# The request order of four weight slabs and one transpose in a two-layer transformer kernel

## Chip, cores, metric

The kernel runs on one core of one Trainium2 chip. The metric is the device time of one execution in microseconds (us).

## The reference, cut to what matters

```python
x = A_x                                              # 2048 tokens x 1024, bf16
x = x + _A_ref(_layernorm(x), A_wqkv, A_wo)          # attention over 8 dilated positions
x = x + _B_ref(_layernorm(x), W_gate, W_up, W_down)  # relu(x Wg) * (x Wu), then Wd; F = 3584
... # both lines once more
```

## The kernel before

The tokens are worked on in blocks of 512, that is, four tiles of 128 rows. Weights come as slabs of 1 MB through a ring of five buffers. The program is written as a list of events with plan times; the events are sorted and emitted, so a plan time settles only the order of instructions on each engine. It isn't a time on the chip. All loads and transposes below are issued by one queue, that of SyncE (SP).

```python
def sp_dma(dst, src, transpose=False):
    start = nc.sync.dma_start_transpose if transpose else nc.sync.dma_start
    ...                                   # each is issued after the one before it

def want_gu(n, at, gap):                  # gate and up slabs, with the time their use ends
    for s in range(NSG):
        cols = slice(s * SLAB, min((s + 1) * SLAB, F))
        end = at + gap * min(4 * (s + 1), FC)
        want(("g", n, s), wg_v[:, :, cols], end)
        want(("u", n, s), wu_v[:, :, cols], end)

def slab_events(events):                  # a slab is asked for when the slab five before it ends
    for i, (key, src, _) in enumerate(slab_plan):
        ...                               # f: takes a ring buffer, sp_dma(tv, src)
        events.append((slab_plan[i - RING][2] + 0.3 if i >= RING else 0.1 * i, f))

def ln2(n, ats, turn_at=None, dve=()):    # second norm: stats, apply, transpose of each tile
    stats, apply, turn, hold = ln_steps(n, "b", False, dve)
    for t, a in enumerate(ats):
        ev.append((a, stats[t]))
        ev.append((a + 4.0, apply[t]))
        if turn_at is None:               # only the first block: one transpose per tile
            ev.append((a + (7.5 if t == TPB - 1 else 6.0), turn(t)))
    ...

# gate and up: every matmul reads the transposed norm of all four tiles
for nm in ("g", "u"):
    for kc in range(KC):
        mm(acc[:], lhsT=slab[(nm, n, s4)][:, kc, jl * P:(jl + 1) * P], rhs=ln["xnT"][:, :, kc, :], ...)

# plan of the stretch in question
want_v("v123", t_v3 + GRP * KC / 2, t_gu0)   # two V slabs, ends 141.3 and 148.2
want_wo(0, t_v3, t_v3)                       # two slabs of the output projection, end 134.3
spread(wo_steps(0), t_wo0, 2 * GRP)
ln2(0, [...], None, (2, 3))                  # tiles 0 and 1 on ScalarE, 2 and 3 on VectorE
spread(v_steps(3, ln_a[3], "v123"), t_v3, GRP)   # V projection of block 3
...                                              # then gate and up of block 0, from t_gu0 on
```

In the text, T0 to T3 are the transposes of the first block's four tiles (256 KB each), g00, g01, g02 the gate slabs 0, 1, 2 of block 0, and u00, u01 its up slabs.

## Time and profile before

| what | value |
|---|---|
| time, median of 3 runs | 1651.05 us (1649.98 to 1651.11) |
| span of the profiled run | 1648.9 us (1648.95 with one more digit) |
| TensorE (PE) busy | 98% |
| its longest wait | 11.0 us, before the first gate matmul |

The page of the kernel before, its first lines (busy us of each engine, share of the span, instructions). PE is TensorE, PEld its weight loads, DVE is VectorE, ACT ScalarE, POOL GpSimd:

```profile
span 1648.9 us, 18636 instructions
PE 1620.7 (98%) x7576; PEld 777.8 (47%) x7576; DVE 1059.4 (64%) x918; ACT 512.2 (31%) x1057; POOL 267.3 (16%) x220
```

PE bounds the kernel, and what can be won by reordering is its idle time. The table of waits of the kernel before, with its PE lines (waiting instruction, releaser, total us, times, longest):

```profile
engine line waited for: us in total, times, longest us
...
PE acc_g L118 <- issue: 11.0, 1, 11.0
PE tp L294 <- DVE xn_first L276: 9.0, 1, 9.0
...
```

The 9.0 us are the start of the program. The 11.0 us are one gap; "issue" says that PE waited for nothing that this profile shows, so the releaser has to be looked for elsewhere. The timeline of PE of the kernel before shows where the gap lies (start, duration, what; idle time before it in brackets):

```profile
135.26 14.17 PE L118 MATMUL acc_v<-xnT_a,w_v 128*128 128x512 bf16 x64
160.44 3.57 PE L118 MATMUL acc_g<-xnT_b,w_g 128*128 128x512 bf16 x8 [11.01 <-issue]
163.81 2.38 PE L118 MATMUL acc_u<-xnT_b,w_u 128*128 128x512 bf16 x8
166.02 1.89 PE L118 MATMUL acc_g<-xnT_b,w_g 128*128 128x512 bf16 x8
```

The V projection ends at 149.43, the first gate matmul starts at 160.44. The first two groups of eight take 5.58 us (160.44 to 166.02), while two later ones take 3.45. The timeline of SP of the kernel before, in the same stretch (start and length of an issue, not of the transfer):

```profile
145.32 1.23 SPq L107 DMA_TRANSPOSE xnT_b<-xn_b  x1
146.65 0.53 SPq L107 DMA_DIRECT2D w_u<-in_B_W_up_dram  x1
147.27 0.59 SPq L107 DMA_DIRECT2D w_g<-in_B_W_gate_dram  x1
147.96 4.41 SPq L107 DMA_TRANSPOSE xnT_b<-xn_b  x1
152.49 0.51 SPq L107 DMA_DIRECT2D w_u<-in_B_W_up_dram  x1
153.10 2.85 SPq L107 DMA_TRANSPOSE xnT_b<-xn_b  x1
156.48 0.38 SPq L107 DMA_DIRECT2D w_g<-in_B_W_gate_dram  x1
```

These are T1, u01, g02, T2, u00, T3, g01. The view of the tile xnT_b, cut to 153 to 156 us, gives T3's time from issue to landing in the kernel before:

```profile
DMA to landing us min/median/max: 7.2/7.2/7.2
```

So T3 lands at 153.10 + 7.2 = 160.3, and PE starts 0.1 us later: T3 ends the gap. Three slabs stand between T1 and T3. The window table of the kernel before gives the clock and the load of the DMA engines (busy time and instructions of PE, PEld, DVE, ACT, POOL; granted clock, that is, the share of full speed at which TensorE was let run; mean share of the 16 DMA engines; GB/s):

```profile
152.00:155.00 3.00, 0.00 (x0) 0.00 (x0) 2.90 (x2) 0.00 (x0) 0.00 (x0) 0.92 1.19 329
155.00:158.00 3.00, 0.00 (x0) 0.00 (x0) 2.96 (x3) 0.00 (x0) 0.00 (x0) 0.50 1.09 320
158.00:161.00 3.00, 0.56 (x2) 0.28 (x3) 3.00 (x2) 0.41 (x1) 0.00 (x0) 0.50 1.15 334
```

The DMA engines are full in these windows (a share of 1.09 to 1.19), so everything that stands ahead of T3 delays it. The clock has fallen to 0.50 by the time PE starts again: this explains the slow first groups (5.58 us, against 3.45 at a clock of 1.00).

### The profile page before, as it was taken

Reading aid. Unit: us, or ns where it says so; the run is one execution under the profiler, and the core shown is the slowest. Engines: PE = TensorE matmul, PEld = TensorE weight load, DVE = VectorE, ACT = ScalarE, POOL = GpSimd, SP = SyncE. Lnnn points to the kernel's source line nnn. Section 1 sums busy time; section 2 is a strip of 40 time slices with the busy share of each in tenths; the row PEclk is TensorE's granted clock in tenths of the full one; section 3 lists DMA queues with packets and bytes.
Section 4 is the critical chain, followed back from the end, with each engine's and each line's share of the span. In section 5 each row is a group of like instructions: output and inputs, shape, how many; then the busy total and the mean of one; then the engine's idle time right before and its main releaser. Section 6 shows DMA issues by size and latency. Waiting matters only on the chain.

```text
span 1648.9 us, 18636 instructions
## 1 busy us (share of the span) xinstructions
PE 1620.7 (98%) x7576; PEld 777.8 (47%) x7576; DVE 1059.4 (64%) x918; ACT 512.2 (31%) x1057; POOL 267.3 (16%) x220
## 2 busy tenths in 40 slices
PE   7997999999999999999999999999999999999999
PEld 4553445444454445444454444544445444444444
DVE  3698988978198844959459493694927948211111
ACT  5833412415132522325124151340513401131110
POOL 1321104401053101211052010520105100000000
PEclk9998999999999999999999999999999999999999
DMA  9558666764747474784747748467485774655451
GB/s 297 90 155 217 159 170 192 206 184 154 229 147 193 148 204 146 229 211 134 211 156 202 197 153 229 154 188 200 153 229 178 186 218 151 204 157 184 153 161 69
DMA packets 371222, 296.81 MB, mean 180 GB/s; under 512 B 142400, under 2 KB 351296, under 8 KB 370240
## 3 DMA queue, kind: packets, MB, share of 16 engines
q1 hardware_dynamic: 370848, 295.10, 62.3%
q8 instruction: 59, 0.97, 0.2%
q10 hardware_dynamic: 288, 0.52, 0.1%
q14 instruction: 27, 0.22, 0.0%
HBM read 256.77 MB, written 21.00 MB: 168 GB/s over the span
## 4 chain that ended last, share of the span: by engine, by line
PE 91%; DVE 3%; ACT 3%; DMA 1%; issue 1%; POOL 1%; SPq 0%; DVEq 0%; ACTq 0%; POOLq 0%
PE acc_g L118 24%; PE acc_u L118 23%; PE dacc L118 23%; PE acc_wo L118 6%; PE acc_k L118 5%; PE acc_q L118 5%; PE acc_v L118 4%; DVE pv L480 1%; DMA x<-in_A_x_dram 1%; DVE pv L481 1%; DVE t L416 1%; DMA xnT_b<-xn_b 1%; ACT xn_a L224 0%; ACT xn_a L225 0%; ACT xn_a L241 0%
## 5 line engine op out<-in xcount | busy, mean ns | idle before, releaser
L118 PE MATMUL acc_g<-xnT_b,w_g 128*128 128x512 bf16 x1792 | 425.1, 380 | 11.0 <-issue 11.0
L118 PE MATMUL acc_u<-xnT_b,w_u 128*128 128x512 bf16 x1792 | 423.8, 379 | 0.0
L118 PE MATMUL dacc<-w_d,hT 128*128 128x512 bf16 x1792 | 388.1, 379 | 0.0
L550 DVE TENSOR_TENSOR hT<-acc_u,r 128x512 bf16<-128x512 f32 x224 | 153.6, 688 | 317.6 <-PE acc_u L118 301.9
L549 ACT ACTIVATE r<-acc_g 128x512 bf16<-128x512 f32 x224 | 132.6, 594 | 699.1 <-PE acc_g L118 690.6
L118 PEld LDWEIGHTS <-w_g 128*128 128x128 bf16 x1792 | 175.0, 98 | 225.0 <-issue 16.1
L118 PEld LDWEIGHTS <-w_u 128*128 128x128 bf16 x1792 | 175.5, 98 | 212.1 <-issue 1.1
L118 PEld LDWEIGHTS <-hT 128*128 128x128 bf16 x1792 | 175.3, 98 | 211.4
L418 DVE TENSOR_TENSOR t<-q,k 128x2048 f32<-128x2048 bf16 x84 | 191.8, 2290 | 9.7 <-ACT k L357 7.0
L428 DVE TENSOR_TENSOR ac<-ac,t 128x2048 f32<-128x2048 f32 x84 | 191.8, 2284 | 0.4
L362 POOL COPY kh<-k 128x14 bf16<-128x14 bf16 x64 | 85.3, 1338 | 448.4 <-ACT k L357 448.4
L577 DVE TENSOR_TENSOR x<-dacc,x 128x512 bf16<-128x512 f32 x64 | 42.5, 688 | 164.7 <-PE dacc L118 164.7
L480 DVE TENSOR_TENSOR pv<-a,vhm 128x4096 bf16<-128x4096 bf16 x64 | 145.3, 2284 | 0.0
L229 POOL TENSOR_TENSOR st_b<-st_b,neg_half 128x1 f32<-128x1 f32 x30 | 65.5, 2187 | 324.6 <-ACT st_b L228 324.6
L118 PE MATMUL acc_wo<-w_o,oT 128*128 128x512 bf16 x512 | 112.0, 379 | 0.2 <-DVE x L525 0.2
L229 POOL TENSOR_TENSOR st_a<-st_a,neg_half 128x1 f32<-128x1 f32 x32 | 48.0, 1499 | 339.6 <-ACT st_a L228 339.6
L118 PEld LDWEIGHTS <-oT 128*128 128x128 bf16 x512 | 50.1, 98 | 60.7 <-issue 0.5
L481 DVE TENSOR_TENSOR pv<-pv 128x2048 bf16<-128x2048 bf16 x64 | 77.5, 1216 | 0.2
L361 POOL COPY k<-kh 128x14 bf16<-128x14 bf16 x48 | 63.8, 1328 | 60.2 <-DVE t L418 43.8
L224 ACT ACTIVATE xn_b<-x 128x1024 bf16<-128x1024 bf16 x30 | 31.3, 1045 | 94.1 <-DVE x L525 94.1
L353 ACT CAST q<-acc_q 128x512 bf16<-128x512 f32 x64 | 37.3, 583 | 68.5 <-PE acc_q L118 68.5
L318 ACT CAST vT<-acc_v 128x512 bf16<-128x512 f32 x64 | 36.9, 587 | 64.9 <-PE acc_v L118 64.9
(125 smaller groups left out, 1206.1 us busy)
## 6 DMA issues: line engine op xcount, KB each, us to landing
w_g<-in_B_W_gate_dram SPq DMA_DIRECT2D x56, 1024.0 KB, 6.8
w_u<-in_B_W_up_dram SPq DMA_DIRECT2D x56, 1024.0 KB, 5.4
w_d<-in_B_W_down_dram SPq DMA_DIRECT2D x48, 1024.0 KB, 5.8
w_o<-in_A_wo_dram SPq DMA_DIRECT2D x16, 1024.0 KB, 7.3
vhm<-v_d SPq DMA_DIRECT2D x32, 284.0 KB, 6.7
v_d<-vT SPq DMA_DIRECT2D x8, 1024.0 KB, 10.2
oT<-o_d SPq DMA_DIRECT2D x32, 256.0 KB, 4.2
w_d<-in_B_W_down_dram SPq DMA_DIRECT2D x16, 512.0 KB, 3.9
```

The source lines that it names most:

```text
L118: tail_pe[0] = nc.tensor.matmul(*args, **kwargs).ins
L229: nc.gpsimd.tensor_tensor(rstd, vpe, neg_half[:, 0:1], op=ALU.pow)
L353: nc.scalar.copy(q[:], acc[:])
L361: nc.gpsimd.tensor_copy(k[:, 0:HALO], khalo[n - 1][:, c, :])
L362: nc.gpsimd.tensor_copy(khalo[n][:, c, :], k[:, BLK:BLK + HALO])
L418: nc.vector.tensor_tensor(t[:], i0, i1, op=ALU.mult)
L428: nc.vector.tensor_tensor(o, ac[:], t[:], op=ALU.add)
L480: nc.vector.tensor_tensor(tt[:], a_bc, v_sh, op=ALU.mult)
L481: nc.vector.tensor_tensor(tt[:, 0:4], tt[:, 0:4], tt[:, 4:8], op=ALU.add)
L549: nc.scalar.activation(r[:], acc[:], ACT.Relu)
L550: nc.vector.tensor_tensor(hold["hT"][:, j, :], accs["u"][:], r[:], op=ALU.mult)
L577: nc.vector.tensor_tensor(xs, ac[t], xs, op=ALU.add)
```

## The change

A slab takes whichever ring buffer is free. The list of plan ends isn't sorted: the output projection's slabs end (134.3) before the V slabs asked for ahead of them (141.3, 148.2). The change asks for each slab at the earliest release that the plan allows, instead of the release of the slab five before it. It also drops the later plan time of T3.

```diff
-            events.append((slab_plan[i - RING][2] + 0.3 if i >= RING else 0.1 * i, f))
+            ends = sorted(end for _, _, end in slab_plan[:i])
+            events.append((ends[i - RING] + 0.3 if i >= RING else 0.1 * i, f))
...
-                ev.append((a + (7.5 if t == TPB - 1 else 6.0), turn(t)))
+                ev.append((a + 6.0, turn(t)))
```

## The prediction

> **What bounds the kernel now.** The page gives PE busy 98% of 1648.9 us. The table of waits has no entry for PE after 165 us; before that PE waits some 13 us in the first 80 us, and has one gap of 11.0 us: the timeline shows the fourth V projection end at 149.4 and the first gate matmul start at 160.44. The window table shows the granted clock at 0.50 from 155 until about 164.7, so the first gate and up groups take 5.6 us instead of 3.5: 2 us more.
>
> **What the change does.** I worked the request times out from the plan. Of 232 slabs four move: u00 and g01 are asked for at plan time 134.6 instead of 141.6 and 148.5; u01 and g02 at 141.6 and 148.5 instead of 134.6. All other ends are already sorted. Besides, the fourth transpose of the second norm moves from 141.9 to 140.4, ahead of the third of these slabs. No operation, byte or buffer is added or removed; the order in SP's queue changes (T is a transpose of 256 KB, a slab 1 MB):
> - before: T1, u01, g02, T2, u00, T3, g01
> - after: T1, u00, g01, T2, T3, u01, g02
>
> **What it costs on the critical path.** The gap ends when T3 lands, since every gate matmul reads all four token tiles. From SP's timeline and the times to landing, issue to landing: T1 145.3 to 148.4; u01 146.65 to 152.35; g02 147.27 to 155.3; T2 147.96 to 156.2; u00 152.49 to 159.3; T3 153.10 to 160.3; g01 156.48 to 163.7. T3's data was ready at 146.3 (DVE timeline): only the queue held it. Landings follow queue order, about 3 us per slab and 1 us per transpose. [...] Two slabs still precede T2, so it lands at about 156.2 as before. But u00's megabyte (156.2 to 159.3) no longer lies between T2 and T3: T3 should land at about 157.3. u00 is in by 152.4, g01 by 155.3; u01 and g02 land at 160 to 163, needed from about 171.
>
> So the gap shrinks to about 8.0 us. The clock falls all the same: it dropped at about 154.7, 5 us into the gap. [...] the slow stretch after the restart (4.3 us here) may differ; I allow -0.5 to +1 us. After 160 us PE has no idle time, so the rest moves forward unchanged: DVE waits 4.2 us for the first hidden tile and finishes s at 204.0, 7 us before PE reads it, so it holds nothing back.
>
> **Predicted:** 1651.05 - 3.0 + 0.2 = about 1648.2 us, 8 in 10 between 1646.8 and 1649.8. Faster by over 2%: 0.01; within 2%: 0.98; slower: 0.01.
>
> **Right if** T3's issue starts at about 152.5 and it lands at about 157.3, PE's gap is near 8 us, and all after it comes 3 us earlier with the same PE busy time. The second hunk does most: with the first alone u01 stands where u00 stood, and the gain should be near nothing.
>
> **Wrong if** T3's issue is held by the full queue for longer, if T2 and T3 slow each other, if the clock recovers later, or if the scheduler reorders other engines.

1651.05 - 3.0 (the gap) + 0.2 (the clock) = 1648.25 us, put down as about 1648.2. The +0.2 and its range of -0.5 to +1 us are my estimate; the measured figure beside it, a slow stretch of 4.3 us after the restart, is from the trace of before.

## The result

The kernel after: median 1648.27 us of 4 runs (1646.56 to 1648.65), before 1650.82 us (1649.98 to 1651.11). The ratio is 0.9983, with a 95% interval from 0.9966 to 1.0001. That interval still touches 1. A later repeat with five rounds gave 1647.75 against 1650.88 us, ratio 0.9981 (0.9968 to 0.9993): the gain is about 3 us and is real.

The page of the kernel after, first lines:

```profile
span 1644.8 us, 18587 instructions
PE 1617.0 (98%) x7527; PEld 777.8 (47%) x7576; DVE 1059.5 (64%) x918; ACT 511.9 (31%) x1057; POOL 264.6 (16%) x220
```

(PE's count is 49 lower because the trace lacks a few records; its weight loads are all there.) The table of waits of the kernel after, its PE lines:

```profile
PE tp L295 <- DVE xn_first L277: 8.9, 1, 8.9
PE acc_g L118 <- DMA xnT_b<-xn_b: 7.8, 1, 7.8
```

The gap has shrunk from 11.0 to 7.8 us, and now the profile itself names the transpose as its releaser. The timeline of PE of the kernel after:

```profile
134.18 14.16 PE L118 MATMUL acc_v<-xnT_a,w_v 128*128 128x512 bf16 x64
156.15 3.57 PE L118 MATMUL acc_g<-xnT_b,w_g 128*128 128x512 bf16 x8 [7.80 <-DMA xnT_b<-xn_b]
159.51 2.54 PE L118 MATMUL acc_u<-xnT_b,w_u 128*128 128x512 bf16 x8
161.88 1.89 PE L118 MATMUL acc_g<-xnT_b,w_g 128*128 128x512 bf16 x8
```

This profile reaches the V projection 1.08 us earlier than that of before (134.18 against 135.26). This is scatter of the start, not the change: over the eleven profiles that point lies between 134.18 and 135.98, and no instruction before it differs in order between the two. So the span (4.1 us shorter) flatters the change. The timeline of SP of the kernel after:

```profile
144.23 1.23 SPq L107 DMA_TRANSPOSE xnT_b<-xn_b  x1
145.56 0.53 SPq L107 DMA_DIRECT2D w_u<-in_B_W_up_dram  x1
146.18 0.59 SPq L107 DMA_DIRECT2D w_g<-in_B_W_gate_dram  x1
146.86 7.15 SPq L107 DMA_TRANSPOSE xnT_b<-xn_b  x2
154.12 0.52 SPq L107 DMA_DIRECT2D w_u<-in_B_W_up_dram  x1
155.17 0.38 SPq L107 DMA_DIRECT2D w_g<-in_B_W_gate_dram  x1
```

The order is T1, u00, g01, T2 and T3 (merged in one line), u01, g02. T3's own landing, from the view of xnT_b from 151.3 to 153.9 us of the kernel after, where its issue starts at 151.34:

```profile
DMA to landing us min/median/max: 4.7/4.7/4.7
```

It lands at 156.05, and PE starts at 156.15. The window table of the kernel after shows the clock falling here too:

```profile
151.00:154.00 3.00, 0.00 (x0) 0.00 (x0) 2.90 (x2) 0.00 (x0) 0.00 (x0) 0.50 1.18 316
154.00:157.00 3.00, 0.85 (x3) 0.34 (x4) 2.96 (x3) 0.71 (x1) 0.00 (x0) 0.50 1.05 237
```

With the same start, the sum is short. Gap: 7.80 - 11.01 = -3.21 us. First two groups: 161.88 - 156.15 = 5.73, before 5.58: +0.15. From the second gate group to the end: 1648.95 - 166.02 = 1482.93 us before and 1644.81 - 161.88 = 1482.93 after. Nothing else changed.

### The profile page after: what moved, and what is told of

The parts are those of the page before. It is cut to its first block, busy times and chain, and to the rows that moved or that the text cites. A ratio compares the mean times of both kernels' runs of the same rounds, so it can differ in the third digit from the quotient of the medians.

```text
span 1644.8 us, 18587 instructions
## 1 busy us (share of the span) xinstructions
PE 1617.0 (98%) x7527; PEld 777.8 (47%) x7576; DVE 1059.5 (64%) x918; ACT 511.9 (31%) x1057; POOL 264.6 (16%) x220
## 4 chain that ended last, share of the span: by engine, by line
PE 91%; DVE 3%; ACT 3%; DMA 1%; issue 1%; POOL 1%; ACTq 0%; SPq 0%; DVEq 0%; POOLq 0%
PE acc_g L118 24%; PE acc_u L118 24%; PE dacc L118 23%; PE acc_wo L118 6%; PE acc_k L118 5%; PE acc_q L118 5%; PE acc_v L118 4%; DVE pv L481 1%; DMA x<-in_A_x_dram 1%; DVE pv L482 1%; DVE t L417 1%; DMA xnT_b<-xn_b 1%; ACT xn_a L225 0%; ACT xn_a L226 0%; ACT xn_a L242 0%
```

## The experiments

Three theories stood at the outset. Q (queue): only the bytes ahead of T3 in SP's queue count. W (weights): the gain comes from u00 and g01 being asked for earlier, as the change intends. N: there is no gain, only scatter. The lines shown are the edit against the kernel before for slabs_only and turn_only, and against the change or the kernel named for the others; all gave correct results, and each was run five times beside nine runs of the kernel before. This table collects what the timelines of PE show. "Slabs" are those issued between T1 and T3. "First two groups" is from the first gate matmul to the start of the second gate group, a wait for u00 included where there is one (turn_only, t_first); it is 3.44 us in early_one, where the granted clock was 1.00, and 3.45 in swap. "Rest" is from there to the end of the span.

| kernel | slabs | gap, us | first two groups, us | rest, us | median, us | ratio to before (95%) |
|---|---|---|---|---|---|---|
| before | 3 | 11.01 | 5.58 | 1482.93 | 1650.88 | |
| after_again | 2 | 7.76 | 5.91 | 1482.93 | 1647.75 | 0.9981 (0.9968 to 0.9993) |
| slabs_only | 3 | 10.95 | 5.98 | 1482.92 | 1650.17 | 0.9996 (0.9984 to 1.0009) |
| turn_only | 2 | 7.71 | 6.15 | 1482.92 | 1648.39 | 0.9986 (0.9974 to 0.9999) |
| one_ahead | 1 | 5.21 | 5.14 | 1482.93 | 1644.62 | 0.9962 (0.9950 to 0.9975) |
| half_ahead | 1/2 | 3.32 | 5.13 | 1483.04 | 1643.12 | 0.9954 (0.9942 to 0.9967) |
| t_first | 0 | 1.95 | 5.45 | 1482.94 | 1641.80 | 0.9948 (0.9934 to 0.9961) |
| early_pair | 0, two before T1 | 3.98 | 4.75 | 1482.93 | 1644.83 | 0.9960 (0.9947 to 0.9972) |
| early_one | 0, one before T1 | 2.18 | 3.44 | 1483.56 | 1640.96 | 0.9939 (0.9925 to 0.9952) |
| swap | 0, one before T1 | 1.57 | 3.45 | 1484.16 | 1640.95 | 0.9940 (0.9927 to 0.9954) |

(The median of the kernel before, in the first line, is that of the first call; beside the later runs it was 1651.13 and 1650.84.)

### The change once more: after_again

Edit: both hunks of the change, written without new lines.

> The changed kernel once more, with the same lines, for a tighter interval. Theory Q (queue order: only the bytes that stand ahead of the fourth transpose T3 in SP's queue count, about 3 us per megabyte slab): PE's gap before the first gate matmul near 7.8 us, time 2.5 to 4 us below before, interval clear of 1. Theory W (weights: the gain comes from slabs u00 and g01 being asked for earlier) and theory N (there is no gain, the 2.6 us is scatter of the start of the kernel, whose first 139 us differed by 1.1 us in the two profiles): N expects a ratio whose interval holds 1.

Measured: gap 7.76 us, 3.1 us less by the medians, and an interval clear of 1. N falls. The start of this profile agrees with that of before (V projection at 135.26 in both), so moments can be compared directly: T3's issue began at 152.47 and it landed at 157.10.

### The first hunk alone: slabs_only

```diff
-            events.append((slab_plan[i - RING][2] + 0.3 if i >= RING else 0.1 * i, f))
+            events.append((sorted(end for _, _, end in slab_plan[:i])[i - RING] + 0.3 if i >= RING else 0.1 * i, f))
```

> First hunk alone: queue T1, u00, g01, T2, u01, T3, g02, so T3 has three slabs ahead of it, as before. Q: T3 lands about 15 us after T1's issue begins, gap 10.5 to 11.5 us, time within 0.7 us of before. W: most of the gain stays, gap near 8 us, time 2 to 3 us below before.

Measured: the gap is 10.95 us, and the time is 0.7 us below before, the edge of what Q allowed, with an interval that holds 1. The timeline of PE of slabs_only:

```profile
134.42 14.17 PE L118 MATMUL acc_v<-xnT_a,w_v 128*128 128x512 bf16 x64
159.54 3.57 PE L118 MATMUL acc_g<-xnT_b,w_g 128*128 128x512 bf16 x8 [10.95 <-issue]
```

Asking for u00 and g01 earlier doesn't shorten the gap by itself: u01 then stands between T2 and T3, where u00 stood. W falls by the gap, which it expected near 8 us; the interval of the time alone would still allow the 2 us of W.

### The second hunk alone: turn_only

```diff
-                ev.append((a + (7.5 if t == TPB - 1 else 6.0), turn(t)))
+                ev.append((a + 6.0, turn(t)))
```

> Second hunk alone: queue T1, u01, g02, T2, T3, u00, g01, so T3 has two slabs ahead of it and u00 comes after it. Q: gap to the first gate matmul 7.5 to 8.2 us; u00 lands about 3 us after T3, when the first gate group (3.4 us at the low clock) is ending, so at most 1 us of wait before the first up group; time 2 to 4 us below before. W: no gain, since u00 and g01 come as late as before: within 0.7 us of before.

The timeline of PE of turn_only:

```profile
134.74 14.17 PE L118 MATMUL acc_v<-xnT_a,w_v 128*128 128x512 bf16 x64
156.62 3.57 PE L118 MATMUL acc_g<-xnT_b,w_g 128*128 128x512 bf16 x8 [7.71 <-DMA xnT_b<-xn_b]
160.71 2.22 PE L118 MATMUL acc_u<-xnT_b,w_u 128*128 128x512 bf16 x8 [0.52 <-DMA w_u<-in_B_W_up_dram]
```

Measured: the gap is that of the change, the late u00 costs a wait of 0.52 us, and the time is 2.5 us below before. So the transpose's plan time carries the gain, and by the profiles the slab hunk adds at most this half microsecond. The medians of turn_only and after_again differ by 0.6 us, which five runs don't resolve.

### All transposes first: t_first

Edit: the change, and u00 and g01 asked for after T3.

```diff
+            events.append(({11: 140.5, 12: 140.6}.get(i) or (sorted(...)[i - RING] + 0.3 ...), f))
```

> All four transposes ahead of all slabs: T0, T1, T2, T3, u00, g01, u01, g02. Q: T3 lands about 5 us after T1's issue begins, gap to the first gate matmul 1 to 2 us; then u00 is late (it lands about 8 us after T1's issue begins) and the first up group waits 1 to 3 us; [...] the clock stays at 1.00 and the 2 us of slow matmuls go too: time 8 to 11 us below before, near 1641. W: slower than the changed kernel, since u00 and g01 come later than in it.

The timeline of PE of t_first:

```profile
135.53 14.17 PE L118 MATMUL acc_v<-xnT_a,w_v 128*128 128x512 bf16 x64
151.65 1.89 PE L118 MATMUL acc_g<-xnT_b,w_g 128*128 128x512 bf16 x8 [1.95 <-issue]
155.37 1.90 PE L118 MATMUL acc_u<-xnT_b,w_u 128*128 128x512 bf16 x8 [1.84 <-DMA w_u<-in_B_W_up_dram]
```

Measured as Q expected: gap 1.95 us, 1.84 us of wait for u00, full clock (1.00; the first gate group takes 1.89 instead of 3.57 us), and 9.1 us less. T3 and u00 landed somewhat later than expected, 6.0 and 9.7 us after T1's issue began instead of 5 and 8. This kernel asks for u00 and g01 later than the changed one and is 6 us faster than it: the opposite of W.

### One slab ahead: one_ahead

Edit: as t_first, with `{12: 140.5}`: g01 goes behind T3, and u00 stays between T1 and T2.

> One slab ahead of the last two transposes: T0, T1, u00, T2, T3, g01, u01, g02. Theory Q (only the bytes ahead of T3 count): the gap so far was 11.0, 7.8 and 1.95 us with three, two and no slabs ahead, so about 4.6 us here. [...] the first gate and up groups should run at full clock and the time should fall by 6.4 us of gap and 2.1 us of slow matmuls: 8 to 9 us below before, near 1642.3. If the clock falls all the same, only by 6.4 us. If the clock had nothing to do with the time (rival C), also only by 6.4.

The timeline of PE of one_ahead:

```profile
135.13 14.17 PE L118 MATMUL acc_v<-xnT_a,w_v 128*128 128x512 bf16 x64
154.50 3.50 PE L118 MATMUL acc_g<-xnT_b,w_g 128*128 128x512 bf16 x8 [5.21 <-DMA xnT_b<-xn_b]
```

Measured: the gap is 5.21 us, 0.6 more than expected, and the clock fell at 154.61, just after PE had restarted; the time fell by 6.5 us and not by 8 to 9. That is the number which the rival C (the clock has nothing to do with the time) gave as well, and Q for the case that the clock falls all the same, so the time alone doesn't decide. The timeline does: the first two groups took 5.14 us here and 3.44 in early_one, so the clock costs 1.7 us in this very run. What falls is the reason I gave for full clock. It was an estimate, read from the kernel before alone, where the clock fell 5.1 us after the last V matmul. In after, after_again, slabs_only and turn_only, all profiled by then, it had fallen after 2.2 to 2.5 us. What the profiles show of it stands below, under "The clock".

### A slab before T1: early_one and early_pair

Between T0 and T1 SP waits about 4 us for ScalarE's normalised tile. Two kernels use this wait. Edits: `{11: 130.95, 12: 140.5}` (u00 there, g01 behind T3) and `{11: 130.95, 12: 130.96}` (both there).

> u00 asked for between T0 and T1, where SP otherwise waits some 5 us for ScalarE, and nothing else until T3 is issued: T0, u00, T1, T2, T3, g01, u01, g02. Q: gap as in the kernel with all transposes first, 1.9 us, but no wait for u00 (1.84 us there), and no fall of the clock: 10.5 to 11.5 us below before, near 1639.8; the best of all so far by 1.5 to 2 us.

> u00 and g01 asked for between T0 and T1: T0, u00, g01, T1, T2, T3, u01, g02. The same bytes stand ahead of T3 as in the changed kernel, but they have 5 us of an otherwise waiting queue to land in. Q in its plain form (bytes ahead of T3 in the queue, wherever) would give a gap near 7.8 us; Q as I hold it (bytes that have not landed when T3 is issued) gives 2 to 3.5 us and 9.5 to 11 us below before.

The timeline of SP of early_one, and after it that of PE:

```profile
140.59 1.23 SPq L107 DMA_TRANSPOSE xnT_b<-xn_b  x1
141.92 0.53 SPq L107 DMA_DIRECT2D w_u<-in_B_W_up_dram  x1
145.92 4.00 SPq L107 DMA_TRANSPOSE xnT_b<-xn_b  x3
```

```profile
152.22 1.89 PE L118 MATMUL acc_g<-xnT_b,w_g 128*128 128x512 bf16 x8 [2.18 <-DMA xnT_b<-xn_b]
153.94 1.89 PE L118 MATMUL acc_u<-xnT_b,w_u 128*128 128x512 bf16 x8
```

Measured for early_one: gap 2.18 us, no wait for u00, full clock (1.00), 10.2 us less than before. That is 1.2 us short of what was expected, and by medians only 0.8 us better than t_first. Half of it is in the "rest" of the table, 0.6 us longer; swap below tells why.

Measured for early_pair: gap 3.98 us, 6.3 us less. Both forms of Q missed the size of the gap (7.8 us, and 2 to 3.5), and the second also the time (9.5 to 11 us less). The reason is in the landings: u00 landed at 147.82, but g01, issued at 142.66, took 8.4 us and landed at 151.07, and the transposes behind it at 151.79, 152.66 and 153.88. A wait of 4 us has room for one slab and not for two. The profiled run was the fastest of its five (1643.53 us; the others 1644.2 to 1644.9, with a mean clock of 0.998 instead of 0.999), so the other four seem to have had more of the slow clock; they weren't profiled at this point.

### Bytes or transfers: half_ahead

Edit: as one_ahead, but u00 in two transfers of half a megabyte, the second behind T3 and ahead of g01 (`{12: 140.6}`).

```diff
+                sp_dma(tv[:, 0:4] if key == ("u", 0, 0) else tv, src[:, 0:4] if key == ("u", 0, 0) else src)
...
+    slab_events(ev); ev.append((140.55, lambda: sp_dma(slab[("u", 0, 0)][:, 4:8], wu_v[:, 4:8, 0:SLAB])))
```

> u00 loaded by two transfers of half a megabyte, the first between T1 and T2, the second after T3: T0, T1, half of u00, T2, T3, other half, g01, u01, g02. If the bytes count (Q), the gap lies half way between the 1.95 us of no slab ahead and the 5.21 of one: 3.3 to 3.9 us. If each transfer ahead costs the same whatever its size (rival D), it is 5.0 to 5.4. The other half lands 1 to 2 us after T3, so the first up group waits little or not. Time for Q: 7.4 us of gap less than before, and 0 to 2 us more for the clock, so 1641.5 to 1644 us; for D 1644 to 1645.

The timeline of PE of half_ahead:

```profile
153.18 2.49 PE L118 MATMUL acc_g<-xnT_b,w_g 128*128 128x512 bf16 x8 [3.32 <-issue]
155.46 3.02 PE L118 MATMUL acc_u<-xnT_b,w_u 128*128 128x512 bf16 x8
```

Measured: 3.32 us, in Q's range and far from D's 5.0 to 5.4. The bytes count. The clock fell here as well, at 154.32, in the middle of the first gate group, though the gap was only 3.32 us.

### The two middle transposes in the other order: swap

Edit: early_one, with T1's plan time at `a + 9.6`, behind T2.

> The kernel with u00 asked for between T0 and T1 once more, with T1 and T2 changed in order (T0, u00, T2, T1, T3, g01): T2's rows come from VectorE, T1's from ScalarE, and T1's were the later by about half a microsecond. The gap of 2.18 us should shrink by 0.3 to 0.6 us; the time by as much, to about 1640.5, which the scatter of the runs will hardly resolve. If the transposes were limited by the transfers and not by their issue, the gap stays 2.2.

The table of waits of swap, its PE lines (cut):

```profile
PE acc_g L118 <- DMA xnT_b<-xn_b: 1.6, 1, 1.6
...
PE acc_u L118 <- DVE hT L550: 1.0, 1, 1.0
```

Measured: the gap shrank by 0.61 us to 1.57, as it should if the issue of the transposes limits them once the queue is empty. The time didn't move (1640.95 against 1640.96 us). PE now waits 1.0 us for VectorE's hT (the product of a gate and an up group), a wait that the kernels before and after don't have; in early_one it is 0.4 us. VectorE still has the products of block 1 to do in this stretch, and PE, which started earlier, runs into it. The next bound is there: the 0.6 us won in the gap came back as 0.6 us more "rest" (1484.16 against 1483.56).

## Why the prediction was right

- **What bounds the gap.** Predicted: T3's landing ends it, and only the queue holds T3 back. Shown by slabs_only, turn_only, one_ahead and t_first: the gap follows the number of slabs between T1 and T3 (11.0, 7.8, 5.2, 1.95 us for 3, 2, 1, 0), whichever slabs they are, and half_ahead shows that it is their bytes. Slabs ahead of T1 count as far as they haven't landed (early_pair, 3.98 us).
- **T3's moments.** Predicted: issue at about 152.5, landing at about 157.3. Measured in after_again, whose start agrees with before: 152.47 and 157.10. The gap was to be 8.0 us and is 7.76 to 7.80. In the profiles of before and after the landings follow the order of the queue, with some 3 us between the landings of two slabs that follow each other (before: 152.37 and 155.32). The issue of a transpose held SP for 1.23 us (T1 before) and, behind two slabs that were still under way, for 4.41 us (T2 before), and SP issued nothing else meanwhile.
- **Which hunk.** Predicted: the second does most, and the first alone next to nothing. Measured: -2.5 us and -0.7 us, of which the second isn't clear of zero. The intent of the change, the earlier request for slabs, saves 0.5 us at most, the wait for u00 that turn_only shows.
- **The clock.** I allowed -0.5 to +1 us and took +0.2; the two profiles of the change show +0.15 and +0.33. The size was right, in part by luck, since the picture behind it was too simple: I read from one profile that the clock falls 5 us into the gap. The window tables give its moments. It fell 2.2 us (after) to 5.3 us (one_ahead) after the last V matmul, and twice after PE had already restarted (one_ahead, half_ahead). It fell in all eight profiles whose gap was 3.32 us or more, and in none of the three with gaps of 1.57, 1.95 and 2.18 us (swap, by its 3.45 us for the first two groups; t_first and early_one, at 1.00). It doesn't follow the length of a wait alone: in t_first, PE's wait for kh in the first block was 2.1 us, and the mean clock from 30 to 60 us was 0.94; in early_one the same wait was 3.5 us, and the mean clock stayed 1.00. The clock came back 2.7 us (early_pair) to 5.1 us (slabs_only) after PE had restarted; from its fall to its return passed 3.4 us in one_ahead and half_ahead, 10.2 in before and after, and 13.6 in slabs_only. What sets these moments wasn't shown.
- **The rest.** Predicted: it moves forward unchanged. Measured: 1482.93 us in both. The argument about VectorE's slack held for 3 us of shift; it no longer held in early_one and swap, where PE came 10 us earlier and waited for VectorE.

Predicted time: 1648.2 us. Measured: 1648.27 and 1647.75 us. That the first agrees to 0.1 us is luck, for the four runs behind it spread over 2.1 us; what is shown is the step of about 3 us.

What stays open: nothing here shows what sets the moment at which the clock falls, so whether a gap of some 2 to 4 us costs the clock couldn't be foretold; no run changed the clock and left the gap as it was; and the start of the program, with a scatter of up to 1.8 us between profiles, wasn't studied.

## What to carry to other kernels

When a queue issues in order and the DMA engines are full, a small transfer that ends a wait has to stand ahead of the large ones that nobody waits for yet: count the bytes ahead of it, not the instructions. Here the DMA engines' share was 1.09 to 1.19 (before, 152 to 161 us), and the gap was 11.0 us with three slabs ahead of the transpose, 3.32 with half a slab and 1.95 with none. Look for moments when the queue itself waits, and put into them what fits; here one slab before T1, with the rest behind T3, made a kernel 10 us faster than before and 7 us faster than the change. Undo each hunk of a change singly: the one that gave it its name may not be the one that works.
